# The last stage of a fused kernel: scatters spread over steps, another order of PSUM banks, and the last groups block by block

## The chip, the core and the metric

The kernel is one program on 1 core of a Trainium2 chip. It is timed in device microseconds, as the median of several executions. The core has five engines, each with an instruction queue that is worked off in order: TensorE (PE, with its weight loads as PEld), VectorE (DVE), ScalarE (ACT), GpSimd (POOL) and SyncE (SP). Matmuls write into PSUM banks of 128 x 512 words of fp32. POOL and DMA read SBUF only, so a finished PSUM bank is first copied to SBUF by ACT or DVE and stored from there. An engine that needs the work of another waits on a semaphore, and everything behind it in its queue waits too.

## The reference, cut to what matters

Attention with a window and some global rows gives 4 x 544 = 2176 rows of 512; a mixture of experts with one expert per row follows; the last part, the only one that the change touches, is a feed-forward block with a rational activation:

```python
def _moe2_ref(x, w_in, w_out, a, b):          # x 2176 x 512, w_in 512 x 2048, w_out 2048 x 512
    h = x @ w_in
    h2 = h * h
    h3 = h2 * h
    P = a[0] + a[1] * h + a[2] * h2 + a[3] * h3
    Q = 1.0 + np.abs(b[0]) * np.abs(h) + np.abs(b[1]) * h2
    g = P / (Q + 1e-06)
    return (g @ w_out).astype(np.float32)
```

The rows come to it sorted by expert, so each finished row is stored by its token number: a scatter.

## The kernel before

All products are made of fp32 numbers that are split into a high and a low part (`gh` and `gl` for g, the two halves of `slot` for the weights); three matmuls (high by high, high by low, low by high) stand for one.

The last stage, `moe2`, cuts the 17 blocks of 128 rows into five chunks of 4, 3, 4, 3 and 3 blocks (`CH`), and each chunk into 16 groups `f` of 128 hidden columns. A pair (chunk, f) is a **step** s, 0 to 79. A step has three parts, which different engines work on at different times:

- `gemm1(s)` on PE: 12 matmuls (L1140) that make h for a step, 128 hidden columns by 512 or 384 rows, in a PSUM bank `ph`. It runs 1 to 3 steps ahead of the activation.
- `elem(s)`, the activation. ACT takes h and makes `ab` (L1242), `u` (L1243) and `q` (L1244); POOL multiplies `q` by `ab` (L1245); ACT makes the reciprocal `r` by Ln and Exp (L1257, L1259); DVE makes `u` from h (L1246, L1247), refines `r` and finishes `u` (L1263, L1266, L1270). In the next `elem` call ACT rounds the finished `u` to `gh` (L1254), and DVE takes the rest `gl` (L1255; on POOL in some steps of the first chunk). ACT's Ln of a step stands in its queue ahead of ACT's three instructions on the next step's h, so POOL's multiply of the next step can't begin before POOL's multiply of this one has gone through ACT.
- `gemm2(s)` on PE: for each of the chunk's blocks i three matmuls (L1282) that add this step's share into the block's own PSUM bank `acc{i}`. It runs 3 steps behind the activation, from step 48 on 4 steps behind (`lag`).

The queues' order is the order in which the loop at the end of `moe2` writes the parts out: in round s first `gemm2(s - lag)`, then `gemm1` as far ahead as it may go, then `elem(s)`.

When the 16th `gemm2` of a chunk has been written out, `elem` of the same round calls `store` behind ACT's Exp: ACT and DVE take turns in copying the chunk's accumulators into the SBUF buffers `raw` (L1297), POOL converts each block's row numbers to integers (`ix`, L1293) and issues one scatter per block (L1299, 128 rows of 2 KB). The four scatters, or three, stand in POOL's queue in one piece, between the multiply of this step and that of the next. The first matmuls of the next chunk write the same accumulators and wait for the copies. Chunks end in rounds 18, 34, 51 and 67 (first to fourth) and in round 83.

Six PSUM banks matter here besides the accumulators: four for h, `bank[0]` to `bank[3]`. In the first chunk only `bank[1]` and `bank[0]` take turns, since ACT puts `r` into `bank[2]` (`bank_r`) and the conversion of the second weight matrix works in `bank[3]` (`bank_f`, L713 to L719). From step 16 on all four take turns:

```python
ph_of = lambda s: bank[(s + 1) % 2] if first_ch(s) else bank[(s + 1) % HB]
```

So steps 16, 17, 18, 19 use banks 1, 2, 3, 0, and so on with a period of four.

Of the kernel before, what the change touches and what calls it, by code (L numbers as in the profile page):

```python
# [11 lines left out]
I32 = mybir.dt.int32  # L12
# [54 lines left out]
TR = (1, 1), (2, 2)  # L67
HB = 4
AY = 14, 11, 2
STE = lambda nc, ch, i: nc.vector.tensor_copy if i % 2 else nc.scalar.copy  # L70
LEAD = 2
YQ = lambda nc: nc.scalar
AQ = lambda nc: nc.gpsimd
# [28 lines left out]
class Build:  # L102
# [1087 lines left out]
    def moe2(self):  # L1190
        nc, tc, out = self.nc, self.tc, self.t["out"]
        with ExitStack() as st:
            P = lambda name, bufs: st.enter_context(tc.tile_pool(name=name, bufs=bufs))
            PP = lambda name, bufs: st.enter_context(tc.tile_pool(name=name, bufs=bufs, space=PSUM))
            qp = P("qp", 1)
# [4 lines left out]
            chunks, t0 = [], 0  # L1200
# [6 lines left out]
            lag = lambda s: SK if s < late else SK + 1  # L1207

            def gbuf(t_, s):
                w, k = (512, SK) if s < late else (384, SK + 1)  # L1210
                return gt[t_][:, w * (s % k):w * (s % k) + chunks[steps[s][0]][1] * 128]
            et = {t_: [qp.tile([128, 512], F32, name=f"{t_}{n}") for n in range(k)] for t_, k in ER.items()}
            Wo = self.slot[1]
            bank = self.bank[::-1] + [ps_h.tile([128, 512], F32, name=f"ph2_{n}") for n in range(HB - PRE)]
            first_ch = lambda s: s < 16
            ph_of = lambda s: bank[(s + 1) % 2] if first_ch(s) else bank[(s + 1) % HB]
            bank_r, bank_f = bank[2], bank[3]

            load_y = lambda ch, i: self.load_y(chunks[ch][0] + i)
            prep = lambda ch, i: self.x2_prep(chunks[ch][0] + i, x2[ch], i, nc.gpsimd if ch == 1 else nc.vector)  # L1220
            steps = [(c, f) for c in range(len(chunks)) for f in range(16)]
            hs, gs, us, accs, out_ = {}, {}, {}, {}, []
            n_steps = len(steps)

            def gemm1(s):
                ch, f = steps[s]
                w = chunks[ch][1] * 128
                hs[s] = ph_of(s) if s > 1 else None
                if s >= 2 + PRE:
                    self.product(hs[s], x2[ch], f, w)  # L1230

            def elem(s):

                if s < 2:
                    g = [x.rearrange("p c (i t) -> p c i t", i=2) for x in self.first_g(s)]
                    gs[s] = [[x[:, i // 2, i % 2] for i in range(4)] for x in g]
                    return
                if s < n_steps:
                    w = chunks[steps[s][0]][1] * 128
                    h = hs.pop(s)[:, :w]  # L1240
                    ab, q, u, r0 = (et[t_][s % len(et[t_])][:, :w] for t_ in ("ab", "q", "u", "r0"))
                    nc.scalar.activation(ab, h, AF.Abs)  # L1242
                    nc.scalar.activation(u, h, AF.Identity, scale=a3, bias=a2)  # L1243
                    nc.scalar.activation(q, ab, AF.Identity, scale=b1, bias=b0)  # L1244
                    nc.gpsimd.tensor_tensor(out=q, in0=q, in1=ab, op=ALU.mult)  # L1245
                    nc.vector.tensor_tensor(out=u, in0=h, in1=u, op=ALU.mult)  # L1246
                    nc.vector.scalar_tensor_tensor(out=u, in0=u, scalar=a1, in1=h, op0=ALU.add, op1=ALU.mult)  # L1247
                    for _ in range(SPN(s)[0]):
                        next(sp, None)
                if 3 <= s <= n_steps:  # L1250
                    g = [gbuf(t_, s - 1) for t_ in ("gh", "gl")]
                    gs[s - 1] = [[x[:, 128 * i:128 * i + 128] for i in range(chunks[steps[s - 1][0]][1])] for x in g]
                    up = us.pop(s - 1)
                    nc.scalar.copy(g[0], up)  # L1254
                    GL(nc, s - 1).tensor_tensor(out=g[1], in0=up, in1=g[0].bitcast(F32), op=ALU.subtract)  # L1255
                if s < n_steps:
                    nc.scalar.activation(r0, q, AF.Ln, bias=eps1)  # L1257
                    r = bank_r[:, :w] if first_ch(s) else r0
                    nc.scalar.activation(r, r0, AF.Exp, scale=-1.0)  # L1259
                if out_:  # L1260
                    store(out_.pop())
                if s < n_steps:
                    nc.vector.scalar_tensor_tensor(out=q, in0=q, scalar=1.0 + 1e-6, in1=r, op0=ALU.add, op1=ALU.mult)  # L1263
                    for _ in range(SPN(s)[1]):
                        next(sp, None)
                    nc.vector.scalar_tensor_tensor(out=r, in0=q, scalar=2.0, in1=r, op0=ALU.subtract, op1=ALU.mult,  # L1266
                                                   reverse0=True)
                    for _ in range(SPN(s)[2]):
                        next(sp, None)
                    nc.vector.scalar_tensor_tensor(out=u, in0=u, scalar=a0, in1=r, op0=ALU.add, op1=ALU.mult)  # L1270
                    us[s] = u

            def gemm2(s):
                ch, f = steps[s]
                t0, n = chunks[ch]
                g = gs.pop(s)
                for i in range(n):
                    if f == 0:
                        accs[i] = ps_a.tile([128, 512], F32, tag=f"acc{i}", name=f"acc{i}")
                    l = [g[a][i] for a in range(2)]  # L1280
                    for j, (a, b) in enumerate(((0, 0), (0, 1), (1, 0))):
                        nc.tensor.matmul(accs[i], lhsT=l[a], rhs=Wo[:, b, f, :], start=(f == 0 and j == 0),  # L1282
                                         stop=(f == 15 and j == 2))

            def store(s):
                ch, f = steps[s]
                t0, n = chunks[ch]
                if f == 15:
                    ix = []

                    def row(i):
                        ix.append(qp.tile([128, 1], I32, tag="ix", name="ix", bufs=6))
                        nc.gpsimd.tensor_copy(ix[-1], self.order[:, t0 + i:t0 + i + 1])  # L1293
                    row(0)
                    for i in range(n):
                        o = self.raw[i][:, 0:512]
                        STE(nc, ch, i)(o, accs[i])  # L1297
                        row(min(i + 1, n - 1))
                        ins = nc.gpsimd.indirect_dma_start(  # L1299
                            out=out, out_offset=bass.IndirectOffsetOnAxis(ap=ix[i], axis=0),  # L1300
                            in_=o, in_offset=None)
                        ins = getattr(ins, "ins", ins)
                        self.tc.declare_no_dep(ins, group="rows", reason="every token has a row of its own")
                        self.tc.add_to_no_dep_group("rows", ins)

            x2 = [self.xa if k % 2 else self.x2c for k in range(len(CH))]
            def w_out():
# [27 lines left out]
                    ahead.setdefault(16 * ch - AY[1] + AY[2] * i, []).append(lambda ch=ch, i=i: prep(ch, i))  # L1335
            n, made = len(steps), []
            fed = []
            for s in range(n + lag(n)):
                def ahead_(s=s):
                    while len(made) < min(n, s + (2 if 2 <= s < 16 else LEAD + 1 + (s >= late))):  # L1340
                        gemm1(len(made))
                        made.append(s)

                if s < 2:
                    ahead_()
                while len(fed) <= s - lag(s):
                    gemm2(len(fed))
                    out_.append(len(fed))
                    fed.append(s)
                if s >= 2:  # L1350
                    ahead_()
                elem(s)
                if s == ORDER:
                    nc.sync.dma_start(out=order, in_=self.toks[0:NT].rearrange("(j p) o -> p (j o)", p=128),
                                      allow_slow_non_contiguous=True)
                if s < n:
                    for do in ahead.get(s, ()):
                        do()


def window(n):
# [86 lines left out]
```

## Time and profile before

| what | value |
|---|---|
| median of 3 runs | 809.46 us (807.95 to 814.21) |
| the profiled execution | 810.68 us; its span, first to last instruction, is 809.2 us |
| mean granted clock of TensorE | 0.996 of full speed |
| busy: PE, PEld | 777.2 us (96%), 667.2 us (82%) |
| busy: DVE, ACT, POOL | 581.9 us (72%), 542.0 us (67%), 378.9 us (47%) |
| the last stage | about 430 us to the end of the span |

Busy is the union of the instructions' times on an engine. The 1.48 us between the profiled execution and its span lie outside the instructions.

### The profile page before, as it was taken

The page shows a single profiled execution, that of the slowest core. Times are in us where ns is not written, and L with a number is a line of the kernel's source. Part 1 is how long each engine was busy: PE and PEld are TensorE (multiplying, and loading weights), DVE is VectorE, ACT ScalarE, POOL GpSimd, SP SyncE. Part 2 cuts the span into 40 slices and gives each one's busy share as a digit, 9 for nine tenths or more (in the row PEclk, how much of TensorE's full clock was granted, in tenths as well). Part 3 has the DMA queues.
Part 4 walks back from the last instruction along what each step waited for, and adds up shares of the span by engine and source line. Part 5 has one row for each costly group of instructions (what it writes and reads, how often), then busy time and mean ns, then how long its engine had stood idle before and what let it go on. Part 6 is the DMA issues. An engine that isn't in the chain of part 4 may idle for free. (4 is left out here: it accounts for less than half of the span.)

```text
span 809.2 us, 17205 instructions
## 1 busy us (share of the span) xinstructions
PE 777.2 (96%) x6188; PEld 667.2 (82%) x6189; DVE 581.9 (72%) x1432; ACT 542.0 (67%) x1218; POOL 378.9 (47%) x427
## 2 busy tenths in 40 slices
PE   8999998999999999999999999999999999999995
PEld 5767766788989999998987887898778898988983
DVE  5768777652838877881349999688878876888784
ACT  4667664563646666652657888678777776878684
POOL 4346455264626676640564877422343224233322
PEclk9999999999999999999999999999999999999999
DMA  8998992465748899982353341100010001000101
GB/s 302 311 313 277 301 295 61 131 197 184 246 147 272 275 325 329 310 288 74 93 181 108 104 112 36 53 27 28 0 40 27 2 0 53 1 1 0 40 2 39
DMA packets 53022, 112.90 MB, mean 140 GB/s; under 512 B 11106, under 2 KB 25186, under 8 KB 50872
## 3 DMA queue, kind: packets, MB, share of 16 engines
q1 hardware_dynamic: 42232, 96.39, 37.1%
q0 software_dynamic: 4208, 9.80, 3.7%
q10 hardware_dynamic: 6480, 5.39, 2.1%
q8 instruction: 58, 0.95, 0.5%
q14 instruction: 44, 0.36, 0.2%
HBM read 96.47 MB, written 19.03 MB: 143 GB/s over the span
## 5 line engine op out<-in xcount | busy, mean ns | idle before, releaser
L1245 POOL TENSOR_TENSOR q<-q,ab 128x384 f32<-128x384 f32 (+1 forms) x78 | 99.1, 1270 | 210.6 <-ACT q L1244 201.6
L1282 PE MATMUL acc<-slot,gh 128*128 128x512 f32 x528 | 166.1, 395 | 3.8 <-ACT gh L1254 2.0
L697 POOL TENSOR_TENSOR slot<-raw,slot 128x512 fp32r<-128x512 f32 x84 | 115.1, 1378 | 62.4 <-ACT slot L693 51.8
L1140 PE MATMUL ph<-x2c,slot 128*128 128x512 f32 (+1 forms) x552 | 125.2, 375 | 3.1 <-PEq L1113 1.7
L1140 PEld LDWEIGHTS ph<-x2c,slot 128*128 128x128 f32 x552 | 100.9, 187 | 22.5 <-DVE u L1247 2.6
L1282 PEld LDWEIGHTS acc<-slot,gh 128*128 128x128 f32 x528 | 98.1, 187 | 25.1 <-ACT gh L1254 2.8
L1282 PE MATMUL acc<-slot,gl 128*128 128x512 f32 x264 | 104.5, 396 | 0.3 <-DVE gl L1255 0.3
L917 PE MATMUL acc<-hT,slot 128*128 128x256 f32 (+1 forms) x768 | 103.5, 285 | 0.0
L917 PEld LDWEIGHTS acc<-hT,slot 128*128 128x128 f32 x768 | 96.4, 189 | 0.2
L693 ACT CAST slot<-raw 128x512 fp32r<-128x512 f32 x144 | 85.5, 620 | 8.4 <-DVE yt L923 7.4
L1257 ACT ACTIVATE r<-q,cab 128x384 f32<-128x384 f32 (+1 forms) x78 | 51.4, 658 | 42.7 <-POOL q L1245 41.6
L1263 DVE SCALAR_TENSOR_TENSOR q<-q,r 128x384 f32<-128x384 f32 (+1 forms) x64 | 38.6, 604 | 51.6 <-ACT r L1259 51.4
L314 POOL TENSOR_SCALAR pr<-ex,r 128x128 f32<-128x128 f32 x128 | 46.7, 377 | 59.3 <-PE sc L261 17.3
L1140 PE MATMUL ph<-xa,slot 128*128 128x384 f32 x384 | 71.9, 336 | 1.8 <-DVE u L1270 1.8
L1140 PEld LDWEIGHTS ph<-xa,slot 128*128 128x128 f32 x384 | 67.7, 188 | 5.0 <-issue 2.2
L1254 ACT CAST gh<-u 128x384 fp32r<-128x384 f32 (+1 forms) x78 | 43.4, 556 | 32.8 <-DVE u L1270 23.2
L697 DVE TENSOR_TENSOR slot<-raw,slot 128x512 fp32r<-128x512 f32 x60 | 52.8, 881 | 15.7 <-ACT slot L693 14.3
L296 ACT ACTIVATE ex<-sm,mx 128x128 f32<-128x128 f32 x128 | 50.3, 395 | 15.0 <-POOL pr L314 6.8
L1282 PEld LDWEIGHTS acc<-slot,gl 128*128 128x128 f32 x264 | 49.4, 187 | 13.0 <-DVE gl L1255 1.0
L1243 ACT ACTIVATE u<-ph,cab 128x384 f32<-128x384 f32 (+1 forms) x78 | 55.3, 709 | 6.4 <-POOL gl L1255 5.4
L1244 ACT ACTIVATE q<-ab,cab 128x384 f32<-128x384 f32 (+1 forms) x78 | 58.1, 745 | 0.0
L1247 DVE SCALAR_TENSOR_TENSOR u<-u,cab,ph 128x384 f32<-128x384 f32 (+1 forms) x78 | 51.9, 665 | 2.8
(228 smaller groups left out, 1519.8 us busy)
## 6 DMA issues: line engine op xcount, KB each, us to landing
raw<-in_w_dram SPq DMA_DIRECT2D x78, 512.0 KB
vw<-in_vw_dram SPq DMA_DIRECT2D x16, 1024.0 KB
r<-in_w_dram SPq DMA_DIRECT2D x18, 512.0 KB
kw<-in_kw_dram SPq DMA_DIRECT2D x16, 384.0 KB
raw<-wf SPq DMA_DIRECT2D x9, 512.0 KB
qt<-in_qT_dram SPq DMA_DIRECT2D x32, 128.0 KB
xbuf<-xrow SPq DMA_DIRECT2D x8, 512.0 KB
ybuf<-yt ACTq DMA_DIRECT2D x7, 512.0 KB
```

The source lines that it names most:

```text
L296: nc.scalar.activation(ex[:, h], src[:, h], AF.Exp, bias=mx[:, h:h + 1], scale=-1.0, accum_out=ssum[:, h:h + 1])
L314: nc.gpsimd.tensor_scalar(out=pr[:, h], in0=ex[:, h], scalar1=r[:, h:h + 1], scalar2=1.0, op0=ALU.mult, op1=ALU.mult)
L693: nc.scalar.copy(hi, r)
L697: eng.tensor_tensor(out=lo[:, c], in0=r[:, c], in1=hi[:, c].bitcast(F32), op=ALU.subtract)
L917: nc.tensor.matmul(acc[m][:, :n], lhsT=W[:, b, 8 + f, 128 * m:128 * m + 128], rhs=hT[f % nh][:, a, :n], start=(f == 0 and i == 0), stop=(f ...
L1140: self.nc.tensor.matmul(ph[:, :w], lhsT=l[a], rhs=r[b], start=(k == 0 and i == 0), stop=(k == 3 and i == 2))
L1243: nc.scalar.activation(u, h, AF.Identity, scale=a3, bias=a2)
L1244: nc.scalar.activation(q, ab, AF.Identity, scale=b1, bias=b0)
L1245: nc.gpsimd.tensor_tensor(out=q, in0=q, in1=ab, op=ALU.mult)
L1247: nc.vector.scalar_tensor_tensor(out=u, in0=u, scalar=a1, in1=h, op0=ALU.add, op1=ALU.mult)
L1257: nc.scalar.activation(r0, q, AF.Ln, bias=eps1)
L1282: nc.tensor.matmul(accs[i], lhsT=l[a], rhs=Wo[:, b, f, :], start=(f == 0 and j == 0), stop=(f == 15 and j == 2))
```

## The change

It has four parts, all in `moe2`.

1. `store` makes the copies as before, but puts each block's row conversion and scatter into a list, `rows`. Each following `elem` takes one from it, right behind POOL's multiply of `q`. This holds for the first four chunks, 14 scatters.
2. From step 16 on the banks of h have another order: banks 1, 0, 3, 2 for steps 16, 17, 18, 19 and so on, again with a period of four.
3. The `gemm2` of the last three steps (77, 78, 79; `LASTS`) are no longer written out step by step. A new function `last` does block 0 for all three steps, copies it, scatters it, then block 1, then block 2.
4. The copy of the last block is cut in two: columns 0 to 255 on ACT, 256 to 511 on DVE.

```diff
-            ph_of = lambda s: bank[(s + 1) % 2] if first_ch(s) else bank[(s + 1) % HB]
+            ph_of = lambda s: bank[(s + 1) % 2] if first_ch(s) else bank[(1, 0, 3, 2)[s % HB]]
...
                     nc.gpsimd.tensor_tensor(out=q, in0=q, in1=ab, op=ALU.mult)
+                    if rows:
+                        rows.pop(0)()
...
-            def gemm2(s):
+            def gemm2(s, blocks=None):
...
+            def row(t0, i):
+                ix = qp.tile([128, 1], I32, tag="ix", name="ix", bufs=6)
+                nc.gpsimd.tensor_copy(ix, self.order[:, t0 + i:t0 + i + 1])
+                return ix
...
             def store(s):
...
-                    row(0)
-                    for i in range(n):
-                        o = self.raw[i][:, 0:512]
-                        STE(nc, ch, i)(o, accs[i])
-                        row(min(i + 1, n - 1))
-                        ins = nc.gpsimd.indirect_dma_start(
...
+                for i in range(n):
+                    (nc.vector.tensor_copy if i % 2 else nc.scalar.copy)(self.raw[i][:, 0:512], accs[i])
+                    rows.append(lambda i=i: scatter(i, row(t0, i)))
+
+            def last():
+                t0, n = chunks[-1]
+                ix = [row(t0, 0)]
+                for i in range(n):
+                    for s in range(n_steps - LASTS, n_steps):
+                        gemm2(s, (i,))
+                    o = self.raw[i][:, 0:512]
+                    if i < n - 1:
+                        (nc.vector.tensor_copy if i % 2 else nc.scalar.copy)(o, accs[i])
+                    else:
+                        nc.scalar.copy(o[:, 0:256], accs[i][:, 0:256])
+                        nc.vector.tensor_copy(o[:, 256:512], accs[i][:, 256:512])
+                    ix.append(row(t0, min(i + 1, n - 1)))
+                    scatter(i, ix[i])
...
-            for s in range(n + lag(n)):
+            for s in range(n + lag(n) - LASTS):
...
+            last()
```

`scatter` holds the indirect DMA that `store` had. The lines of `elem` behind the new two stand two further down in the changed kernel (L1246 became L1248).

On POOL, at the end of the fourth chunk (round 67), the queue before; `q0` and `q1` are the multiplies of steps in turn, `ix` the row numbers, `out_0_dram` the scatters:

```order
L1245 TENSOR_TENSOR q1_8402<-q1_8402,ab0_8400 128x384
L1293 CAST ix_10941<-order_8413 128x1
L1293 CAST ix_10944<-order_8413 128x1
L1299 DMA out_0_dram<-raw0_74,ix_10941 2176x512
L1293 CAST ix_10948<-order_8413 128x1
L1299 DMA out_0_dram<-raw1_75,ix_10944 2176x512
L1293 CAST ix_10952<-order_8413 128x1
L1299 DMA out_0_dram<-raw2_76,ix_10948 2176x512
L1245 TENSOR_TENSOR q0_8401<-q0_8401,ab0_8400 128x384
```

and in the changed kernel:

```order
L1245 TENSOR_TENSOR q0_8401<-q0_8401,ab0_8400 128x384
L1287 CAST ix_10969<-order_8413 128x1
L1291 DMA out_0_dram<-raw0_74,ix_10969 2176x512
L1245 TENSOR_TENSOR q1_8402<-q1_8402,ab0_8400 128x384
L1287 CAST ix_11006<-order_8413 128x1
L1291 DMA out_0_dram<-raw1_75,ix_11006 2176x512
L1245 TENSOR_TENSOR q0_8401<-q0_8401,ab0_8400 128x384
L1287 CAST ix_11043<-order_8413 128x1
L1291 DMA out_0_dram<-raw2_76,ix_11043 2176x512
```

The scatters, which stood together between two multiplies, now stand one behind each of the next three multiplies; the fourth, unused row conversion is gone.

On PE, at the seam of the first two chunks (round 16), the products of steps 17 and 18 stand in a row; `ph2_0` is bank 2, `ph2_1` is bank 3, and `ph_8026` is bank 0. The piece of the difference:

```order
 L1282 MATMUL acc3_8442<-slot1_3338,gh_8398 128x512 x2
 L1282 MATMUL acc3_8442<-slot1_3338,gl_8399 128x512
-L1140 MATMUL ph2_0_8406<-xa_3342,slot0_81 128x384 x12
+L1140 MATMUL ph_8026<-xa_3342,slot0_81 128x384 x12
 L1140 MATMUL ph2_1_8407<-xa_3342,slot0_81 128x384 x12
```

Nothing moved but the bank that the first of the two writes: step 17's product goes to bank 0, which step 15's h had, in place of bank 2, which step 15's `r` had.

At the end of the program, PE's last step before, and PE's last rows now (`acc0` to `acc2` are the blocks):

```order
L1282 MATMUL acc0_10958<-slot1_3338,gh_8398 128x512 x2
L1282 MATMUL acc0_10958<-slot1_3338,gl_8399 128x512
L1282 MATMUL acc1_10962<-slot1_3338,gh_8398 128x512 x2
L1282 MATMUL acc1_10962<-slot1_3338,gl_8399 128x512
L1282 MATMUL acc2_10966<-slot1_3338,gh_8398 128x512 x2
L1282 MATMUL acc2_10966<-slot1_3338,gl_8399 128x512
```

```order
L1282 MATMUL acc1_10945<-slot1_3338,gh_8398 128x512 x2
L1282 MATMUL acc1_10945<-slot1_3338,gl_8399 128x512
L1282 MATMUL acc2_10949<-slot1_3338,gh_8398 128x512 x2
L1282 MATMUL acc2_10949<-slot1_3338,gl_8399 128x512
L1282 MATMUL acc2_10949<-slot1_3338,gh_8398 128x512 x2
L1282 MATMUL acc2_10949<-slot1_3338,gl_8399 128x512
L1282 MATMUL acc2_10949<-slot1_3338,gh_8398 128x512 x2
L1282 MATMUL acc2_10949<-slot1_3338,gl_8399 128x512
```

and DVE's last rows, each with the semaphores that it waits for, before and now (`raw2` is the last block's buffer):

```order
L1263 SCALAR_TENSOR_TENSOR q1_8402<-q1_8402,r00_8405 128x384 [waits Activation_49,Pool_49]
L1266 SCALAR_TENSOR_TENSOR r00_8405<-q1_8402,r00_8405 128x384 [waits DVE_49]
L1270 SCALAR_TENSOR_TENSOR u1_8404<-u1_8404,cab_69,r00_8405 128x384 [waits DVE_49]
L1255 TENSOR_TENSOR gl_8399<-u1_8404,gh_8398 128x384 [waits PE_49,Activation_49]
L1297 COPY raw1_75<-acc1_10962 128x512 [waits DMASW3_49,PE_49]
```

```order
L1268 SCALAR_TENSOR_TENSOR r00_8405<-q1_8402,r00_8405 128x384 [waits DVE_49]
L1272 SCALAR_TENSOR_TENSOR u1_8404<-u1_8404,cab_69,r00_8405 128x384 [waits DVE_49]
L1257 TENSOR_TENSOR gl_8399<-u1_8404,gh_8398 128x384 [waits PE_49,Activation_49]
L1312 COPY raw1_75<-acc1_10945 128x512 [waits DMASW3_49,PE_49]
L1315 COPY raw2_76<-acc2_10949 128x256 [waits DMASW4_49,Activation_49]
```

On PE the last step's blocks stood one after the other; now each block has all three of its last steps before the next block begins. DVE got the last block's second half, which waits for ACT (ACT has the first half), not for PE.

## Rows read from the trace of the kernel before

**Rows 1.** Waits, PE, 430 us to the end: total us, times, longest us.

```profile
PE acc L1282 <- ACT gh L1254: 2.0, 2, 1.1
PE acc L1282 <- ACT raw L1297: 1.9, 2, 1.6
PE ph L1140 <- DVE u L1270: 1.8, 1, 1.8
```

**Rows 2.** Timeline at the seam of chunks 1 and 2: start, length, instruction [idle before].

```profile
497.17 0.75 DVE L1247 SCALAR_TENSOR_TENSOR u<-u,cab,ph 128x512 f32<-128x512 f32 x1
...
500.60 0.68 DVE L719 SCALAR_TENSOR_TENSOR io<-raw,ph 128x512 int32<-128x512 int32 x1
...
502.08 4.41 PE L1140 MATMUL ph<-xa,slot 128*128 128x384 f32 x24 [1.81 <-DVE u L1270]
```

**Rows 3.** Timeline at the end of the third chunk (round 51).

```profile
676.66 0.72 ACT L1244 ACTIVATE q<-ab,cab 128x384 f32<-128x384 f32 x1
...
681.84 1.02 POOL L1245 TENSOR_TENSOR q<-q,ab 128x384 f32<-128x384 f32 x1
```

**Rows 4.** Timeline at the end of the fourth chunk (round 67).

```profile
742.34 0.40 PE L1282 MATMUL acc<-slot,gl 128*128 128x512 f32 x1
...
743.51 1.17 POOL L1245 TENSOR_TENSOR q<-q,ab 128x384 f32<-128x384 f32 x1 [2.83 <-ACT q L1244]
...
745.36 0.52 ACT L1259 ACTIVATE r<-r 128x384 f32<-128x384 f32 x1
745.79 1.06 ACT L1297 COPY raw<-acc 128x512 f32<-128x512 f32 x2
...
746.41 0.74 PE L1282 MATMUL acc<-slot,gh 128*128 128x512 f32 x2 [1.58 <-ACT raw L1297]
...
746.74 0.51 ACT L1242 ACTIVATE ab<-ph 128x384 f32<-128x384 f32 x1
...
747.68 0.72 ACT L1244 ACTIVATE q<-ab,cab 128x384 f32<-128x384 f32 x1
...
748.53 0.99 POOL L1299 DMA_INDIRECT out_dram<-raw,ix  x1 [0.16 <-POOL ix L1293]
...
750.89 1.03 POOL L1245 TENSOR_TENSOR q<-q,ab 128x384 f32<-128x384 f32 x1
```

**Rows 5.** Lines L1299 and L1293: shortest, median, longest ns.

```profile
L1299 POOL DMA_INDIRECT out_dram<-raw,ix x17: 985/999/1316, 513.8 to 805.0; - x17
...
L1293 POOL CAST ix<-order x22: 175/193/556, 511.2 to 804.6; 128x1 int32<-128x1 f32 x22
```

**Rows 6.** Timeline of the last 17 us.

```profile
792.60 0.63 PE L1282 MATMUL acc<-slot,gh 128*128 128x512 f32 x2
...
793.30 0.63 PE L1282 MATMUL acc<-slot,gh 128*128 128x512 f32 x2
...
799.15 0.51 ACT L1254 CAST gh<-u 128x384 fp32r<-128x384 f32 x1 [2.00 <-DVE u L1270]
...
799.71 0.74 PE L1282 MATMUL acc<-slot,gh 128*128 128x512 f32 x2 [1.09 <-ACT gh L1254]
...
800.84 0.59 ACT L1297 COPY raw<-acc 128x512 f32<-128x512 f32 x1 [1.18 <-PE acc L1282]
...
801.81 0.40 PE L1282 MATMUL acc<-slot,gl 128*128 128x512 f32 x1
802.22 1.03 POOL L1299 DMA_INDIRECT out_dram<-raw,ix  x1 [6.03 <-ACT raw L1297]
...
804.96 0.99 POOL L1299 DMA_INDIRECT out_dram<-raw,ix  x1 [0.16 <-POOL ix L1293]
```

**Rows 7.** Lines by form, 430 us to the end: busy us, mean ns, idle before.

```profile
L1246 DVE TENSOR_TENSOR u<-ph,u 128x384 f32<-128x384 f32 x48 | 26.4, 551 | 0.0
...
L1297 ACT COPY raw<-acc 128x512 f32<-128x512 f32 x10 | 5.5, 580 | 2.6 <-PE acc L1282 2.6
L1297 DVE COPY raw<-acc 128x512 f32<-128x512 f32 x7 | 4.8, 689 | 3.5 <-PE acc L1282 3.5
```

More of the change, by code (lines that the diff above doesn't have):

```diff
@@ L69 @@
 AY = 14, 11, 2
-STE = lambda nc, ch, i: nc.vector.tensor_copy if i % 2 else nc.scalar.copy
+LASTS = 3
 LEAD = 2
@@ L1221, in moe2 @@
             steps = [(c, f) for c in range(len(chunks)) for f in range(16)]
-            hs, gs, us, accs, out_ = {}, {}, {}, {}, []
+            hs, gs, us, accs, out_, rows = {}, {}, {}, {}, [], []
             n_steps = len(steps)
@@ L1271, in elem @@
                     us[s] = u
-            def gemm2(s):
+            def gemm2(s, blocks=None):
                 ch, f = steps[s]
-                t0, n = chunks[ch]
-                g = gs.pop(s)
-                for i in range(n):
+                for i in range(chunks[ch][1]) if blocks is None else blocks:
                     if f == 0:
                         accs[i] = ps_a.tile([128, 512], F32, tag=f"acc{i}", name=f"acc{i}")
-                    l = [g[a][i] for a in range(2)]
+                    l = [gs[s][a][i] for a in range(2)]
                     for j, (a, b) in enumerate(((0, 0), (0, 1), (1, 0))):
@@ L1283, in gemm2 @@
                                          stop=(f == 15 and j == 2))
-            def store(s):
[L1286 to L1293, printed above, removed]
-                    row(0)
-                    for i in range(n):
-                        o = self.raw[i][:, 0:512]
-                        STE(nc, ch, i)(o, accs[i])
-                        row(min(i + 1, n - 1))
-                        ins = nc.gpsimd.indirect_dma_start(
[L1300 to L1304, printed above, removed]
+            def row(t0, i):
+                ix = qp.tile([128, 1], I32, tag="ix", name="ix", bufs=6)
+                nc.gpsimd.tensor_copy(ix, self.order[:, t0 + i:t0 + i + 1])
+                return ix
@@ new lines, in scatter @@
+            def scatter(i, ix):
+                ins = nc.gpsimd.indirect_dma_start(
+                    out=out, out_offset=bass.IndirectOffsetOnAxis(ap=ix, axis=0),
+                    in_=self.raw[i][:, 0:512], in_offset=None)
+                ins = getattr(ins, "ins", ins)
+                self.tc.declare_no_dep(ins, group="rows", reason="every token has a row of its own")
+                self.tc.add_to_no_dep_group("rows", ins)
+            def store(s):
+                t0, n = chunks[steps[s][0]]
+                for i in range(n):
+                    (nc.vector.tensor_copy if i % 2 else nc.scalar.copy)(self.raw[i][:, 0:512], accs[i])
+                    rows.append(lambda i=i: scatter(i, row(t0, i)))
@@ L1347, in moe2 @@
                     gemm2(len(fed))
-                    out_.append(len(fed))
+                    if steps[len(fed)][1] == 15:
+                        out_.append(len(fed))
                     fed.append(s)
```

## Prediction

> **What bounds the kernel now.** I read the busy shares first: TensorE is busy for 96% of the span, at nearly its full granted clock. So in the last stage a wait on another engine costs time only where it ends as a wait of PE, or lies behind PE's last matmul. The list of PE's waits then says what there is to win: 1.8 us in one wait on DVE's `u` (L1270), 1.9 us in two waits on ACT's copies, of which one is 1.6, and 2.0 us in two waits on `gh` [rows 1]. The timeline shows where they are.
>
> The wait on `u` is at the seam of chunks 1 and 2: PE stands for 1.81 us, until 502.08, before the products of steps 17 and 18 [rows 2]. The wait of 1.58 us on a copy is at the end of the fourth chunk, at 746.41 [rows 4]; the other, 0.3 us, is at the end of the second. The waits on `gh` lie in the last 14 us, the last of them 1.09 us until 799.71 [rows 6].
>
> The third view is the timeline of POOL around a chunk's end. ACT had `q` of step 68 ready at 748.40 (747.68 + 0.72), but POOL began its multiply at 750.89, behind three scatters [rows 4]. In round 51, with four scatters, `q` was ready at 677.38 and taken at 681.84 [rows 3]. From 750.89 to the end the activation never makes this up: ACT and POOL take turns on `q` and `r`, one step after the other, down to the last `gh`, and PE waits for that.
>
> **The change part by part.** The sum is made in the time of the profiled execution (span 809.2 us, execution 810.68 us, the median of the runs 809.46 us).
>
> *Banks.* Step 17's product no longer waits for `r` of step 15 but for DVE's last read of h of step 15, L1247, done at 497.17 + 0.75 = 497.92. PE is free for it at 502.08 - 1.81 = 500.27, so nothing holds it. What is late next is step 18's product in bank 3: DVE's last conversion there reads it until 500.60 + 0.68 = 501.28, but half of the 4.41 us for both products lies ahead, so PE asks for it at about 502.5 [rows 2]. All 1.81 us are won, and as PE's list has only the 0.3 us wait between there and 744 us, they last [rows 1]. Bounds: 0 and 1.81; I take 1.81. The later order has the same period of four and costs nothing; the reads of h that free a bank lie a whole step earlier.
>
> *Scatters.* 14 of them, each with its row conversion, move past one to four multiplies of `q`. A pair costs POOL 0.19 + 0.16 + 0.99 = 1.34 us, by the longest rows 0.56 + 0.16 + 1.32 = 2.04 [rows 4, 5]. POOL idles 2.83 us before a multiply of 384 columns [rows 4]. So they hide behind POOL's wait for ACT. If a scatter also paid the 0.79 us that POOL took from the end of ACT's copy (801.43) to its first scatter (802.22) [rows 6], the longest would be 2.83, just the slot; but here its data are ready long before. I take 0 per scatter and keep 0.79 for the range. DMA landing is no matter: `raw` is written again only 16 steps later.
>
> What that gives at round 51: `q` of step 52 ends at 677.38 + 0.05 + 1.17 = 678.60 in place of 682.86, 4.2 us earlier; the 0.05 is the step from one engine to the next (`gh` ends at 799.66, PE starts at 799.71), the 1.17 an undisturbed multiply [rows 3, 4, 6]. Those 4.2 us reach round 67, where ACT's Exp ended at 745.88 and would at 741.7. Now ACT's second copy can't start before the chunk's last matmul, 742.34 + 0.40 = 742.74: PE is the late one there, and its 1.58 us wait goes, as goes the 0.3 us one before [rows 4]. By the old distances (0.95 us from the first of two copies to the next `ab`, so 0.47 for one) `ab` of step 68 starts at 743.25 in place of 746.74, `q` is ready at 744.9, and POOL is through at 746.13 in place of 751.92: **5.79 us** earlier, by PE's clock of before [rows 4]. The steps to the end are the same, so the last `gh`, which ended at 799.66, ends at 793.87 [rows 6].
>
> *Last groups.* PE reached step 77 at 792.60; without the 1.58 us wait at 791.02. Three matmuls take 0.70 us (792.60 to 793.30), so 0.233 each; the nine of the last step took 2.50 us from their first start at 799.71 to their last end, 0.4 of it start-up [rows 6]. In the new order block 0's steps 77 and 78 end at 792.4, and its step 79 waits for `gh` until 793.92. From there on 21 matmuls are left and not 9: 2.50 + 12 x 0.233 = 5.30 us, so PE ends at 799.22 and not at 802.21. The gain is 2.99 us; the new order by itself gives back 2.80 of what the earlier `gh` brings.
>
> *The tail.* Before, the last scatter started 2.75 us after PE's end (804.96 - 802.21), since the first two, 1.37 us apart, stood ahead of it [rows 6]. Now block 1 is done 2.1 us before block 2, so POOL is free. What is left: ACT's half copy, DVE's half copy behind it, and 0.79 us to the scatter. A quarter less columns saves DVE 0.13 us (0.551 against 0.689), so half saves about 0.26 by estimate: 0.33 us on ACT, 0.43 on DVE [rows 7]. With 0.05 ahead of each that is 0.05 + 0.33 + 0.05 + 0.43 + 0.79 = 1.65 us, a gain of 1.10. No row of before shows two halves. From below, were they side by side, it would be 1.27; from above, each as long as a whole copy, 2.16. I take them in turn, since DVE's half waits for ACT in the order of the changed kernel; nothing is queued behind it on DVE, and the last scatter waits for it. The scatter itself and the 3.25 us behind it stay.
>
> A rule beside that: the Trainium skill, PSUM — Partial Sum Buffer, section "PSUM bank collisions raise a hardware error", says that no two engines may access one bank in the same partition at once, so the halves of one accumulator can't overlap. By this rule 1.65 stands; without it the sum would be 0.38 us better. No run so far shows it.
>
> *Sum:* 1.81 + 0.3 + 2.99 + 1.10 = **6.2 us**. The span becomes 803.0, the profiled execution 804.5, and the median 809.46 - 6.2 = **803.3 us**.
>
> **The rivals.**
>
> *The end binds (slower).* The 2.80 us of the new last order are paid whenever the last `gh` is what PE waits for, and the tail gives back 1.10. If the last `gh` comes less than 1.7 us earlier on the wall clock than before, the kernel is slower; if it comes at the old time, because the scatters fill POOL's slots and the seam's wait only moves, the time is 809.46 + 2.80 - 1.10 = 811.2 us. For it speaks that PE waits for `gh` already [rows 1, 6]; against it that a median pair of conversion and scatter fills half of the slot [rows 4, 5].
>
> *The seam's wait only moves.* Step 18's product, or DVE's queue behind it, holds PE as long: 803.3 + 1.8 = 805.1 us. Against it stand the two ends of reads, 497.92 and 501.28 [rows 2].
>
> *The scatters don't fit.* They now run beside DVE's work on two SBUF operands, at another place in the step. If each of the three behind round 67 holds the next `q` by 0.79 us, the last `gh` is 2.4 us later: 805.7 us. For it speaks the spread of 985 to 1316 ns for a scatter and 175 to 556 for a conversion, against it the medians near the lower end [rows 5]. The Trainium skill, SBUF — State Buffer, section "Who interferes with whom", says that DVE's two-port modes lock GpSimd out of a shared port for a whole instruction, and its section "SBUF: two separate sides" that this stops the making of DMA descriptors. No row here shows such a lock on a scatter: 1.32 us is the longest.
>
> *The activation is no longer the end.* If the last `gh` comes so early that PE never waits in the last three steps, PE runs on from 791.02 with 27 matmuls, 6.3 us and 0.2 for the last to drain, to 797.5, another 1.7 us: 801.6 us. Against it stands that the steps from 68 on start from PE's own end of round 67 and keep their length.
>
> **How the numbers follow.** Forecast 0.66; seam 0.10; scatters 0.10; early end 0.10; slower 0.04. Range: down to the early end less the 0.38 us of overlapping halves, 801.2, and up to the scatters' 805.7, which also holds the seam. About 1% (8.1 us) is what a measurement of this kernel tells from no change. Faster by more than that means under 801.4: the low side of the early end, and the runs' own spread (807.95 to 814.21), together 0.17. Slower by over 1% needs 817.6, which no case gives: 0.02. Within 1%: 0.81.
>
> **What would show it.** Right: no wait of PE near 502 and near 745 us; a scatter of about 1 us between each two multiplies behind a chunk's end, with the next `q` unheld; one wait of PE for `gh`, ahead of block 0's last three matmuls, and 18 without a gap behind it; DVE's half copy behind ACT's; the last scatter 1.6 us after PE's end. Wrong: a wait of PE on DVE at step 18; ACT's Ln waiting longer for POOL in rounds with a scatter; a last `gh` that sets the end more than 5.3 us before PE's last matmul.

## The result and the profile after

The changed kernel took 801.23 us, the median of 17 runs (798.48 to 806.14); the kernel before, run beside it, 808.09 us (17 runs, 806.02 to 814.21). The ratio is 0.9914, 95% interval 0.9896 to 0.9932: a gain of 0.7 to 1.0%, some 6.9 us. The forecast, 803.3 us from a median of 809.46, is a ratio of 0.9923, a gain of 0.77%.

The profiled span fell from 809.2 to 799.1 us. Not all of that is the change: executions differ by some us ahead of the last stage too, where the two programs are the same. So all comparisons of traces below use one **length**: from the start of DVE's last conversion of the second weight matrix (the L719 row in [rows 2], 500.60 before) to the end of the span. It was 809.2 - 500.6 = 308.6 us before; after, the conversion starts at 497.3, and it is 799.1 - 497.3 = 301.8. That is 6.8 us less, where the prediction had 6.2. (Its start, the **mark**, lies just ahead of PE's wait at the seam, so that wait counts.)

The busy times of the page after:

```profile
PE 774.7 (97%) x6188; PEld 666.9 (83%) x6189; DVE 582.6 (73%) x1433; ACT 542.6 (68%) x1218; POOL 378.7 (47%) x423
```

They hardly moved: DVE, ACT and POOL are within 0.7 us of before, PE within 2.5. What is gone is mostly waits.

PE's waits from 430 us on, as in [rows 1]:

```profile
PE acc L1282 <- ACT gh L1256: 1.5, 1, 1.5
PE ph L1140 <- DVE u L1249: 1.1, 2, 0.8
```

The wait at the seam and both waits on ACT's copies are gone; of the two waits on `gh` one is left. The second row lies in the first chunk, which the change doesn't touch. The timeline after, at the four places of [rows 2, 3, 4, 6], one group for each:

```profile
496.84 4.34 PE L1140 MATMUL ph<-xa,slot 128*128 128x384 f32 x24
497.32 0.68 DVE L719 SCALAR_TENSOR_TENSOR io<-raw,ph 128x512 int32<-128x512 int32 x1
...
670.82 0.72 ACT L1244 ACTIVATE q<-ab,cab 128x384 f32<-128x384 f32 x1
671.62 1.45 POOL L1245 TENSOR_TENSOR q<-q,ab 128x384 f32<-128x384 f32 x1 [4.00 <-ACT q L1244]
673.01 0.18 POOL L1287 CAST ix<-order 128x1 int32<-128x1 f32 x1
673.47 1.20 POOL L1291 DMA_INDIRECT out_dram<-raw,ix  x1 [0.28 <-POOL ix L1287]
675.90 1.16 POOL L1245 TENSOR_TENSOR q<-q,ab 128x384 f32<-128x384 f32 x1 [1.23 <-ACT q L1244]
...
736.46 0.40 PE L1282 MATMUL acc<-slot,gl 128*128 128x512 f32 x1
736.89 0.59 ACT L1301 COPY raw<-acc 128x512 f32<-128x512 f32 x1 [0.34 <-PE acc L1282]
739.11 1.02 POOL L1245 TENSOR_TENSOR q<-q,ab 128x384 f32<-128x384 f32 x1 [4.23 <-ACT q L1244]
740.87 1.03 POOL L1291 DMA_INDIRECT out_dram<-raw,ix  x1 [0.28 <-POOL ix L1287]
742.96 1.17 POOL L1245 TENSOR_TENSOR q<-q,ab 128x384 f32<-128x384 f32 x1 [1.07 <-ACT q L1244]
744.54 1.21 POOL L1291 DMA_INDIRECT out_dram<-raw,ix  x1 [0.28 <-POOL ix L1287]
746.97 1.16 POOL L1245 TENSOR_TENSOR q<-q,ab 128x384 f32<-128x384 f32 x1 [1.22 <-ACT q L1244]
749.27 1.03 POOL L1291 DMA_INDIRECT out_dram<-raw,ix  x1 [1.01 <-POOL ix L1287]
...
787.39 0.51 ACT L1256 CAST gh<-u 128x384 fp32r<-128x384 f32 x1 [2.00 <-DVE u L1272]
787.95 0.74 PE L1282 MATMUL acc<-slot,gh 128*128 128x512 f32 x2 [1.52 <-ACT gh L1256]
792.84 0.40 PE L1282 MATMUL acc<-slot,gl 128*128 128x512 f32 x1
793.28 0.37 ACT L1314 COPY raw<-acc 128x256 f32<-128x256 f32 x1 [3.61 <-PE acc L1282]
793.68 0.42 DVE L1315 COPY raw<-acc 128x256 f32<-128x256 f32 x1 [1.81 <-ACT raw L1314]
794.89 0.98 POOL L1291 DMA_INDIRECT out_dram<-raw,ix  x1 [1.05 <-DVE raw L1315]
```

Steps 17 and 18 start without a wait (no bracket on the first row). In rounds 52 and 68 POOL's idle before each multiply of `q` ends on ACT and not on a scatter: the multiply takes `q` 0.08 us after it is ready (671.62 - 670.82 - 0.72), where it was 4.46 us in round 52 before. At the end of the fourth chunk ACT's copy waits for PE, and not PE for the copy. And at the end 21 matmuls follow the last `gh`, the half copies stand one behind the other, and the last scatter starts 1.65 us after PE's end (794.89 - 793.24).

The scatters and row conversions, shortest, median and longest ns, as in [rows 5]:

```profile
L1291 POOL DMA_INDIRECT out_dram<-raw,ix x17: 982/1200/1322, 513.5 to 794.9; - x17
...
L1287 POOL CAST ix<-order x18: 177/180/648, 512.7 to 793.6; 128x1 int32<-128x1 f32 x18
```

### The profile page after: what moved, and what is told of

It reads as the page before. It is cut to its first block, busy times and chain, and to the rows that moved or that the text cites. A ratio compares the mean times of both kernels' runs of the same rounds, so it can differ in the third digit from the quotient of the medians.

```text
span 799.1 us, 17197 instructions
## 1 busy us (share of the span) xinstructions
PE 774.7 (97%) x6188; PEld 666.9 (83%) x6189; DVE 582.6 (73%) x1433; ACT 542.6 (68%) x1218; POOL 378.7 (47%) x423
```

## The experiments

Each kernel is the changed one with the edit shown, so a part is taken out by undoing it. The kernels e1 to e4 ran beside one set of runs of the kernel before (median 808.88), e5, e6, e8 and e9 beside a second (808.20), e7, e10 and e11 beside a third (809.79). Each ratio is to the kernel before that ran beside it, with its 95% interval. "Expected" is what was put down ahead of the run.

### One part undone

**The old end** (e1_last_by_step): the last steps again step by step, the last copy whole.

```diff
-LASTS = 3
+LASTS = 1
...
-                    if i < n - 1:
-                        (nc.vector.tensor_copy if i % 2 else nc.scalar.copy)(o, accs[i])
-                    else:
-                        nc.scalar.copy(o[:, 0:256], accs[i][:, 0:256])
-                        nc.vector.tensor_copy(o[:, 256:512], accs[i][:, 256:512])
+                    (nc.vector.tensor_copy if i % 2 else nc.scalar.copy)(o, accs[i])
```

> The changed kernel with its last three steps in the old order, step by step, and the last copy whole; scatters and banks stay changed. Measure: the stretch from the start of DVE's last weight conversion (L719) to the end of the span, which is 308.6 us before and 301.8 us in the changed kernel. Theory (the new last order gives PE 2.8 us more work behind the last gh, and its tail gives back 1.1): PE no longer waits at step 79, its end comes 1.5 to 1.9 us earlier than in the changed kernel, the last scatter 2.75 us behind PE's end in place of 1.65, so a stretch of 301.0 to 301.4 us, 0.4 to 0.8 less than the changed kernel, ratio to before 0.991. Rival (the new last order is a gain, because the three scatters no longer queue at the end): PE's end as in the changed kernel, the tail 1.1 longer, a stretch of 302.9 us.

799.99 us, ratio 0.9894 (0.9862 to 0.9926); length 301.0. The end of its timeline, PE's last matmul and the last scatter:

```profile
790.94 0.39 PE L1282 MATMUL acc<-slot,gl 128*128 128x512 f32 x1
...
794.08 0.99 POOL L1291 DMA_INDIRECT out_dram<-raw,ix  x1 [0.16 <-POOL ix L1287]
```

PE never waits for `gh` here. From the mark (497.3) it ends at 791.33 - 497.3 = 294.0, after at 793.24 - 497.3 = 295.9: the block-by-block order costs 1.9 us of PE, the shorter tail (1.65 against 794.08 - 791.33 = 2.75) gives back 1.1. The new end is a loss of 0.8 us in this trace; the timed intervals of the two kernels overlap.

**Scatters in one piece** (e2_scatter_at_once):

```diff
+                ix = [row(t0, 0)]
                 for i in range(n):
                     (nc.vector.tensor_copy if i % 2 else nc.scalar.copy)(self.raw[i][:, 0:512], accs[i])
-                    rows.append(lambda i=i: scatter(i, row(t0, i)))
+                    ix.append(row(t0, min(i + 1, n - 1)))
+                    scatter(i, ix[i])
```

> The changed kernel with the scatters of the first four chunks in one piece as before; banks and last order stay changed. Theory (the scatters carry the late activation, and the new last order costs 1.7 us net when the last gh is late): PE waits for the copies at the end of chunk 4 again (1.6 us) and 3.5 to 4.5 us for gh at step 79; the stretch from DVE's last weight conversion to the end is 308.6 - 1.8 + 2.8 - 1.1 = 308.5 us, ratio to before 1.000. Rival (the banks and the last order bring the gain, the scatters little): 301.8 to 305.7 us, ratio 0.991 to 0.996.

813.34 us, ratio 1.0052 (1.0034 to 1.0070): slower than before. Length 311.7, so 3.2 us over what was expected. PE's waits show the first cause, the timeline and the windows the second. (A row of the windows has the stretch, its length, the busy us of PE, PEld, DVE, ACT and POOL, and then TensorE's granted clock as a share of full speed.)

```profile
PE acc L1282 <- ACT gh L1256: 4.7, 2, 2.5
PE acc L1282 <- ACT raw L1302: 3.4, 2, 1.9
```

```profile
584.31 0.73 PE L1282 MATMUL acc<-slot,gh 128*128 128x512 f32 x2 [1.87 <-ACT raw L1302]
...
796.72 1.22 PE L1282 MATMUL acc<-slot,gh 128*128 128x512 f32 x2 [2.49 <-ACT gh L1256]
```

```profile
789.00:793.00 4.00, 1.78 (x8) 1.17 (x7) 3.28 (x7) 3.21 (x7) 1.22 (x2) 1.00 0.00 0
793.00:796.50 3.50, 0.98 (x3) 0.22 (x2) 2.41 (x5) 1.47 (x3) 0.20 (x2) 0.72 0.00 0
796.50:800.00 3.50, 3.28 (x8) 2.61 (x9) 0.56 (x1) 0.75 (x2) 0.22 (x1) 0.50 0.00 0
```

What PE won at the seam it lost at the end of the second chunk, in a wait of 1.87 us on a copy that was 0.28 before: the copy stands in ACT's queue behind the activation, and that is held by POOL as before. And around two waits for `gh`, 2.22 and 2.49 us, TensorE's granted clock fell to half, from 2.4 to 1.2 GHz: it was full until 793.00, and by its mean of 0.72 up to 796.50 it fell before PE's second wait ended at 796.72. The 21 matmuls took 803.99 - 796.72 = 7.27 us in place of 5.29.

**The old banks** (e3_old_banks):

```diff
-            ph_of = lambda s: bank[(s + 1) % 2] if first_ch(s) else bank[(1, 0, 3, 2)[s % HB]]
+            ph_of = lambda s: bank[(s + 1) % 2] if first_ch(s) else bank[(s + 1) % HB]
```

> The changed kernel with the old order of banks. Theory: the wait of 1.8 us ahead of the products of steps 17 and 18 is back and nothing later absorbs it: a stretch of 301.8 + 1.8 = 303.6 us, ratio to before 0.9938. Rival (a later wait swallows it, since the end hangs on the last gh): 301.8 us, ratio 0.9914.

804.18 us, ratio 0.9939 (0.9919 to 0.9959), as expected; length 305.4, 1.8 us more than expected. The wait is back, and the products behind it took longer than in [rows 2], with the granted clock at half:

```profile
501.32 6.01 PE L1140 MATMUL ph<-xa,slot 128*128 128x384 f32 x24 [1.78 <-DVE u L1272]
```

```profile
501.00:503.00 2.00, 1.68 (x7) 1.71 (x8) 1.26 (x3) 1.83 (x4) 2.00 (x3) 0.70 0.00 0
503.00:505.00 2.00, 2.00 (x8) 2.00 (x7) 1.92 (x3) 0.00 (x0) 0.92 (x1) 0.50 0.00 0
```

6.01 - 4.41 = 1.6 us lie there. Behind the same wait the clock stayed full in the trace before.

### One part alone

**The scatters** (e8_only_scatters): both edits of e1 and e3.

> The kernel before with the spread scatters alone: the banks in the old order, the last three steps step by step, the last copy whole. Lengths are from the start of DVE's last conversion of the second weight matrix to the end of the span: 308.6 us before, 301.8 changed, 301.0 with the old end alone. Theory: the spread scatters carry nearly all of the gain, and the banks 1.8 us, since PE's wait at the seam comes back: 302.8 us, ratio about 0.993; if the granted clock falls behind that wait, as it did with the old banks before, up to 304.6. PE has no wait near the end of the fourth chunk, and the last gh needs no wait or a short one. Rival (the scatters are worth little without the other banks): 306 us or more, ratio 0.997 or above.

802.43 us, ratio 0.9926 (0.9913 to 0.9940); span 798.6, mark 495.6, length 303.0. PE's whole list of waits of the last stage:

```profile
PE ph L1140 <- DVE u L1272: 1.7, 1, 1.7
PE ph L1140 <- DVE u L1249: 0.4, 1, 0.4
```

Nothing on copies, nothing on `gh`. The rival is out: the scatters alone win 5.6 us, where all parts together win 6.8.

**The banks** (e9_only_banks): the edits of e1 and e2.

> The kernel before with the other order of banks alone: scatters in one piece, the old end. Theory from the run with scatters in one piece: the 1.8 us that PE wins at the seam it loses again in a wait on ACT's copies at the end of the second chunk (1.87 us there in place of 0.28) and in gh at the end, since POOL's scatters keep the activation where it was: 308.2 to 308.6 us against 308.6, ratio about 1.000. Rival (the terms of the prediction add up): 306.8 us, ratio 0.998.

808.52 us, ratio 1.0000 (0.9986 to 1.0013); length 308.2. PE at the end of the second chunk and its waits:

```profile
582.55 0.73 PE L1282 MATMUL acc<-slot,gh 128*128 128x512 f32 x2 [1.91 <-ACT raw L1302]
```

```profile
PE acc L1282 <- ACT raw L1302: 3.5, 2, 1.9
PE acc L1282 <- ACT gh L1256: 1.9, 2, 1.1
```

The seam's 1.8 us are gone from the list, and 1.6 us more stand on the copies. The terms do not add up.

**The end** (e6_only_last): the edits of e2 and e3.

> The kernel before with the block-by-block end and the halved last copy alone: old banks, scatters in one piece. Theory: the last gh comes when it did, 21 matmuls stand behind it and not 9 (+2.8 us), the tail gives back 1.1: 310.3 us against 308.6, ratio 1.002; if the granted clock falls in the longer wait for gh, as it did with the other banks and scatters in one piece, up to 312.3, ratio 1.0045. Rival (block by block gains by itself, since the tail is shorter): 307.5 us, ratio 0.9986.

811.97 us, ratio 1.0040 (1.0021 to 1.0058); length 312.8. PE waits 2.26 and 2.50 us for `gh`, and the granted clock is 0.50 from 797 to 803 us; the 21 matmuls take 7.81 us (797.20 to 805.01). Without those 2.5 us it would be 310.3, the theory's number.

### How far the scatters must be spread

**All in one piece, one step later** (e5_all_next_step):

```diff
-                    if rows:
+                    while rows:
                         rows.pop(0)()
```

> The changed kernel with all scatters of a chunk in one piece, but behind the next step's multiply of q and not ahead of it. Theory: three pairs of conversion and scatter take 3 x 1.37 = 4.1 us and POOL's slot before a multiply of 384 columns is 2.83, so the multiply after that is held by about 1.3 us, and what comes late is the last gh: 303.1 us against 301.8 changed, ratio 0.993; behind the chunks of four blocks 2.7 us, which the room in the later steps may take up. Rival (one slot holds them, it is only the place behind the next multiply that counts): 301.8 us, ratio 0.9914.

810.23 us, ratio 1.0023 (1.0007 to 1.0039); length 310.6. Both expectations missed by far. The timeline of ACT and POOL in rounds 52 and 53:

```profile
673.88 1.44 POOL L1245 TENSOR_TENSOR q<-q,ab 128x384 f32<-128x384 f32 x1 [3.99 <-ACT q L1244]
...
675.73 1.20 POOL L1291 DMA_INDIRECT out_dram<-raw,ix  x1 [0.28 <-DVE u L1249]
...
677.36 0.70 ACT L1244 ACTIVATE q<-ab,cab 128x384 f32<-128x384 f32 x1
677.52 1.13 POOL L1291 DMA_INDIRECT out_dram<-raw,ix  x1 [0.28 <-POOL ix L1287]
...
680.58 0.98 POOL L1291 DMA_INDIRECT out_dram<-raw,ix  x1 [0.28 <-issue]
681.58 1.03 POOL L1245 TENSOR_TENSOR q<-q,ab 128x384 f32<-128x384 f32 x1
```

Four pairs took 675.26 to 681.56, 6.3 us or nearly 1.6 each, not 1.37, and `q` of step 53, ready at 678.06, was taken at 681.58: held for 3.5 us. (Behind the fourth chunk three pairs held a `q` for 2.85 us, since the third scatter started 1.01 us after its conversion.) Nor was there room in later steps: a held step is not made up, as in the kernel before. So the last `gh` started 795.04 - 498.3 = 296.7 us from the mark, 1.8 us earlier than before (799.15 - 500.6 = 298.5) and 6.6 later than after (787.39 - 497.3 = 290.1). To that come 1.7 us of the new end and 2.1 us of a clock that fell behind a wait of 2.5 us: 308.6 - 1.8 + 1.7 + 2.1 = 310.6.

**Two to a step** (e10_two_per_step):

```diff
-                    if rows:
+                    for _ in range(min(2, len(rows))):
                         rows.pop(0)()
```

> The changed kernel with up to two scatters behind each multiply of q in place of one: 2 and 2 behind the chunks of four blocks, 2 and 1 behind those of three. Theory: what the kernel with all scatters in one piece lost is POOL's slot of about 2.83 us, and a pair of conversion and scatter costs about 1.5 us where its data are ready (6.35 us for four in that run). Two pairs take 3.0 to 3.3 us, so each double step holds the next multiply by 0.2 to 0.5 us and by no more: against 301.8 us from DVE's last conversion of the second weight matrix to the end of the span (the changed kernel), 302.3 to 303.8, ratio 0.992 to 0.994. Rival (any bundle of scatters upsets the activation, by something other than its own time): near the 310.6 us of the kernel with all in one piece, ratio 1.00.

801.71 us, ratio 0.9910 (0.9880 to 0.9939); length 800.7 - 497.1 = 303.6. It is the scatters' own time that holds `q`: ready at 675.57, taken at 676.17, 0.6 us later, and in the next step at once. The last `gh` comes 0.3 us later than after (787.53 - 497.1 = 290.4); the other 1.5 us are the clock, which fell to 0.50 behind PE's wait of 1.90 us for it. The timed ratio can't tell this kernel from the changed one.

### The end

**A whole last copy** (e7_whole_copy): the second piece of e1's edit alone.

> The changed kernel with the last block's accumulator copied whole by ACT, not in two halves. Theory: the halves went one after the other (0.37 and 0.42 us, 1.65 us from PE's end to the last scatter), so a whole copy of 0.58 us on one engine leaves out a step to the next engine and about 0.2 us: 1.44 us from PE's end to the last scatter, 301.6 us where the changed kernel has 301.8, ratio 0.991. Rival (half copies help, as two engines share the work): 302.0 us or more.

802.98 us, ratio 0.9919 (0.9896 to 0.9943), which can't tell 0.2 us; by the traces the length is 799.8 - 498.2 = 301.6, and the last scatter starts 1.40 us after PE's end (795.56 - 794.16). The halves cost 0.25 us there and win nothing.

**Two steps block by block, whole copy** (e4_two_last_whole, then e11_two_last_again):

```diff
-LASTS = 3
+LASTS = 2
```

with e7's edit.

> The changed kernel with only the last two steps done block by block, and the last block copied whole by ACT. Theory: step 77 in the old order fills PE's 1.5 us wait for the last gh; PE ends about 1.4 us earlier than in the changed kernel, and the last scatter starts 1.43 us after PE's end in place of 1.65 (0.05 + 0.59 + 0.79), or 1.37 behind the second scatter: a stretch of 300.2 to 300.4 us, 1.4 to 1.6 less than the changed kernel, ratio to before 0.9897. Rival (the new last order's length behind gh does not matter): 301.6 us, only the whole copy's 0.2.

> The changed kernel with two of the last steps block by block in place of three, and the last block copied whole, measured a second time beside the others. Theory: PE runs through to the end with next to no wait for gh, and the last scatter starts 1.44 us behind it: 300.2 us where the changed kernel has 301.8, ratio 0.988 to 0.990. Rival (its first ratio of 0.987 was luck of four runs, and the end with three steps is as good): 301.6, ratio 0.991.

First 799.04 us, ratio 0.9872 (0.9835 to 0.9908), then 800.12 us, ratio 0.9875 (0.9853 to 0.9896); length 300.2 both times. PE has next to no wait for `gh` any more, and the last scatter starts 1.44 us after its end. This version beats the kernel before. Over the changed one it wins 1.6 us by two traces; of the timed intervals the first overlaps that of the changed kernel and the second just touches it.

### The eight together

The lengths of all combinations, and in brackets those without what the half clock cost in that trace (the group of matmuls behind the wait, against the same group at the full clock):

| | old end | new end |
|---|---|---|
| old banks, scatters in one piece | 308.6 | 312.8 (310.3) |
| new banks, scatters in one piece | 308.2 | 311.7 (309.7) |
| old banks, scatters spread | 303.0 | 305.4 (303.8) |
| new banks, scatters spread | 301.0 | 301.8 |

Spread scatters win 5.6 to 7.9 us; the banks win 2.0 with them and 0.4 without (by the bracketed lengths of the new end 2.0 and 0.6); the new end loses 0.8 with them and 1.5 to 1.7 without. Each length rests on one trace, but they repeat well: in all five traces with the new banks and spread scatters (after, e1, e4, e7, e11) the last `gh` starts 290.0 to 290.1 us from the mark.

## Why the prediction was right, and where not

**What bounds the kernel.** Right. The waits of the list were the places, and POOL's scatters ahead of the next `q` were the cause of those on the copies and on `gh`: they go when the scatters alone are spread (e8).

**Banks.** The step is right in the changed kernel: the 1.8 us are won, with no new wait of step 18. "They last" was true only because the scatters moved too: in e9 1.6 us of them are lost again at the end of the second chunk, and the banks alone win 0.4 us by the traces and nothing by the timed runs. The prediction read the next wait in PE's list, 0.3 us, as all that could stand in the way; a wait that is 0.3 us long is also the place that has no room for an earlier PE.

**Scatters.** Zero per scatter was right, and its reason too: there is room for one. The price was mis-sized: a pair takes 0.18 + 0.28 + 1.20 = 1.66 us by medians, not 1.34. The conversion now stands right ahead of its scatter, and 0.28 us lie between them where 0.16 did when another scatter lay between. The scatter itself takes 1.20 us by median and not 1.00; why, no run shows. The pair fits the slot of 2.83 us once and not twice (e10) or four times (e5). The changed `q` in round 52 was taken at once, as forecast; so was the one behind the fourth chunk, 3.27 us from PE's last matmul to the end of POOL's multiply (736.86 to 740.13) for a forecast of 3.39.

**Last groups.** PE's wait was forecast as 1.52 us (792.4 to 793.92) and is 1.52; the 21 matmuls as 5.30 and are 5.29. But the 2.99 us in the sum stood under a heading that they don't belong to: they are what the scatters win, less a loss. In the old order PE would not have waited at all (e1, e8), so the rival called the early end (801.6 us, 1.7 below the forecast) describes the kernel without this part, e1; it measured a length 0.8 us below the changed one. By the traces the third and the fourth part of the change together lose 0.8 us.

**The tail.** 1.65 us, to the hundredth, which is partly luck: the half copies take 0.37 and 0.42 us for an estimate of 0.33 and 0.43, and that came from two different operations of DVE [rows 7], used for ACT too. They went one after the other, as this kernel's semaphores make them, which the rule cited from the Trainium skill (PSUM — Partial Sum Buffer, "PSUM bank collisions raise a hardware error") asks for; two reads side by side were not tried, so no run tests the rule.

**The sum.** 6.8 us by the traces for 6.2. PE ended 5.7 us earlier from the mark (301.6 to 295.9) for 5.1; the tail gave the 1.1. Some 0.5 of the rest was there at the end of round 67 (PE's last matmul ended 242.1 us from the mark before and 239.5 after, 2.6 us apart for 1.81 + 0.3). PE's starts show where it arose: at the two waits themselves. Step 17's products started 1.48 us behind the mark before and 0.48 ahead of it after: 1.96 us won for a term of 1.81. The second wait, in the trace before:

```profile
587.24 0.72 PE L1282 MATMUL acc<-slot,gh 128*128 128x512 f32 x2 [0.28 <-ACT raw L1297]
```

The same pair of matmuls starts at 581.49 after and takes 0.63 us. From the marks that is 86.64 and 84.17 us, 2.47 apart, so another 0.51 us were won in its start and 0.1 in its length, for a term of 0.3. The list counts a wait from the end of the last matmul's record, which is 0.40 us long; without a wait the next matmul starts 0.23 us behind the start of the last [rows 6]. So each of these waits cost PE 0.15 to 0.33 us more than the idle time that the prediction took for its price. The last 0.1 is the last `gh`, 5.88 us earlier by PE's clock for a forecast of 5.79 (799.66 - 742.74 against 787.90 - 736.86).

**The step that failed** is in "How the numbers follow": "About 1% (8.1 us) is what a measurement of this kernel tells from no change." The runs told 0.18% from no change, half the width of the ratio's interval, so the forecast's own sum, 0.77%, was a clear gain, and it stood with 0.81 under "within 1%" as if it were none. The measured 0.86% is within 1% and yet not the same time. The prediction gives no working for its 1%; the only spread that it had was that of three runs, 6 us. Single runs of either kernel spread by 8 us, and the ratio of two medians of 17 is much firmer than that. In the sum itself the mechanism held, and the terms that were mis-sized are PE's waits at the seam and on the copies: 1.81 + 0.3 us, which measured 2.6.

**The rivals.** The seam's wait did not move in the changed kernel, and the scatters fit: the longest took 1.32 us, as before. *The end binds* is shown as a mechanism by e2 and e6: with the scatters in one piece the kernel is slower than before, by 0.4 to 0.5%. Its price was too low, 1.7 us; the half clock behind the longer waits put 2.0 to 2.5 us on top.

## What to carry to other kernels

Here a scatter was work of the engine that issued it: it held POOL for 0.98 to 1.32 us, so a burst of them between two steps of a chain held the chain, and one to a step, in POOL's own idle slot, cost nothing. Look for that slot before you place such an issue. Gains at two waits in a row need not add up: the time won at the seam was lost again at the next copies until their cause was moved as well. Run the parts alone and together. Doing the last groups block by block shortened the tail but left more work behind the last operand, so take only as many steps as still leave PE without a wait (two here, not three). And when a forecast says how small a change can be measured, work that out from the spread and the number of runs.

## What the runs showed of the hardware that was not expected

TensorE's granted clock fell from full to half (2.4 to 1.2 GHz) for 3 to 7 us around short waits of a PE that had been busy nearly all the time: 1.90 us (e10), 1.78 us (e3), and pairs of 2.2 to 2.5 us (e2, e5, e6), at a price of 1.5 to 2.5 us each. Behind 1.52 us after the change, and behind 1.81 us in the trace before, 1.87 us in e2 and 1.91 us in e9 (both at the end of the second chunk), it stayed full. So a wait of PE can cost nearly twice its own length, and the length alone does not tell whether it will; what does stays open.

In the traces of before, e3, e4 and e11 the clock also fell ahead of the last stage, where all these programs are the same: before, it was 0.50 from 130.00 to 133.30 us, behind a wait of 1.50 us. In these four the mark lies at 499.8 to 501.3 us, in the other nine at 495.6 to 498.3. That goes some way to tell why executions of one program differ.

The falls are also one reason why the lengths of single traces differ from the timed ratios, each against the kernel before, by up to 2.3 us (e10). By the timed ratios e2, e5 and e6 take 11.2, 8.8 and 10.2 us more than the changed kernel, nearer to their lengths with the fall (9.9, 8.8, 11.0) than without; e3 takes 2.0 us more and e10 0.3 less, nearer to theirs without (2.0 and 0.3 more). So the falls in e3 and e10 may be those of one execution. With intervals of 1.5 us either way that is a hint, not shown, and e4 and e11, whose traces have no fall behind the mark, differ by 2.0 and 1.7 us too.

The third scatter behind the fourth chunk started 1.01 us after its conversion in all nine kernels whose scatters stand behind a multiply, where the others behind a multiply wait 0.28. It held nothing after the change; its cause stays open.
